# Decayed block attention ahead of two gated feed-forward stages: products of 64x64x64 in the four quarters of TensorE's array

## The chip, the cores and the metric

The kernel runs on one core of a Trainium2 chip. The metric is the time of one execution on the device, in microseconds (us). TensorE (PE) multiplies, VectorE (DVE) and ScalarE (ACT) move results out of its accumulators (PSUM), GpSimd (POOL) does element-wise work between buffers, SyncE (SP) issues the large loads, and 16 DMA engines carry them. "PEld" in a row is PE's load of the stationary operand.

## What is computed

The first part is a decayed attention over blocks of 64 tokens, with a running state per head; its output is the input of a gated feed-forward stage and of a stage of eight experts. Only the first part is touched. Cut to that part, the reference is:

```
B, H, S, D = 2, 8, 768, 64            # block = 64
Dmask = where(rel >= 0, lam ** rel, 0)            # rel = i - j inside a block
for b in range(S // 64):
    intra = (q_b @ k_b.T * Dmask) @ v_b
    inter = (q_b * lam ** (i + 1)) @ kv_state
    out_b = intra + inter
    kv_state = lam ** 64 * kv_state + (k_b * lam ** (63 - i)).T @ v_b
x = out in rows of H * D = 512                    # 1536 tokens
x = (silu(x @ w_gate) * (x @ w_val)) @ w_out
out = experts(x)
```

## The kernel before

The kernel is one program without a loop; the order of the code is the order of each engine's queue (`tc.manual_schedule()`). The attention walks over 12 **units**. A unit is a chunk of 128 tokens of one of the two batches, all 8 heads; units of the two batches alternate. Since a decayed recurrence may be cut at any block length, the kernel uses blocks of 128 tokens. Heads are handled in four pairs; a pair fills 128 rows (2 heads x 64).

For a unit:

- `load` (L227) fetches q, k and v, each 128 tokens x 8 heads x 64 values, 256 KB, by one DMA from SP's queue (L233; k of unit 0 in two halves). Each of the three has 5 buffers. The load of unit u+5 stands at the end of iteration u.
- `em_T` (L285) transposes q and k pair by pair on PE (L295), ACT copies the result out (L297, tile `tT`), DVE scales q by the powers of lam (L301, `qd`), and POOL scales k (L304, `kd`).
- `em_S` (L307) forms the scores of each head (L315: 64 rows of the array, 128 columns), and DVE multiplies them by the decay mask (L318, tiles `at0`, `at1`), two times 512 wide.
- `em_O` (L325) forms the update of the state (L332, `pu`), the state's part of the output (L343) and the scores' part (L347: 128 rows, 64 columns of the array) in one bank `po`. ACT writes the high part of the output `x1[0]` (L353), DVE the rest `x1[1]` (L356) and the new state (L361, L363), of which only the two diagonal 64x64 blocks of each pair are kept; POOL prepares `tmp`, the old state times lam (L335).

All these operands are f32, and a product of f32 shows as two MATMULs and two LDWEIGHTS in the trace. The main loop runs T(u+1), O(u), S(u+1) for the first five units, then T(u+2), S(u+1), O(u). In units 5, 7, 9, 11 the calls `bg_begin()` and `bg(n)` interleave the preparation of the first weights of the feed-forward stage: steps L166, L153, L159, L160, L173 rebuild f32 from the words of a wider type, L141 and L149 split them in a high and a low part. `pump_dma` (L102) fetches one further piece of weights (512 KB). The decay mask `dec` and the powers `lrep` come from two scans on DVE (L260, L269), whose inputs are `lam_b` (lam on all partitions) and `lam_s` (lam of the pair's head on each half of the partitions); three DMAs from ACT's queue bring these (L238, L240), a fourth `wr`, the router's weights.

After the last unit `em_GV` begins: 24 MATMULs of 128x512 per block (L204), 12 for the gate, 12 for the value, first over the 512 first tokens of batch 0. It needs the prepared pieces of weights, and from then on PE works without a gap.

Of the kernel before, what the change touches and what calls it, by code (L numbers as in the profile page):

```python
# [20 lines left out]
def decayed_attention_two_moes(  # L21
# [14 lines left out]
    nc = tc.nc  # L36
# [176 lines left out]
    lam_s = const.tile([P, NP], F32, name="lam_s")  # L213
# [7 lines left out]

    att = ExitStack()
    ap = att.enter_context(tc.tile_pool(name="ap", bufs=1, side="right", reuse_waits="tile"))
    units = [(c, b) for c in range(NCH) for b in range(B)]
    qkv = {}

    def load(u):  # L227
        c, b = units[u]
        for n, src in enumerate((q, k, v)):
            t = ap.tile([P, H, D], F32, tag=f"in{n}", name=f"in{n}", bufs=5)  # L230
            w = H // 2 if u == 0 and n == 1 else H
            for h in range(0, H, w):
                nc.sync.dma_start(out=t[:, h:h + w, :],  # L233
                                  in_=src[b, h:h + w, c * P:(c + 1) * P, :].rearrange("h s d -> s h d"))
            qkv[u, n] = t

    load(0)
# [6 lines left out]
    load(1)  # L244
    load(2)
    load(3)
    load(4)
    nc.scalar.dma_start(out=wr, in_=w_router.rearrange("(k p) e -> p k e", p=P))


    dec = ap.tile([P, 2, NP, P], F32, name="dec")
    lrep = ap.tile([P, NP, P], F32, name="lrep")
    d0 = rawp.tile([P, 2, NP, P], F32, tag="raw", name="raw")
    d1 = rawp.tile([P, 2, NP, P], F32, tag="raw", name="raw")
    nc.vector.tensor_copy(out=d0, in_=lam_b.rearrange("j (p x) -> j x p", x=2).unsqueeze(3).to_broadcast([P, 2, NP, P]))
    nc.vector.memset(d0[:, :, :, 0:1], 0.0)
    for x in range(2):
        nc.gpsimd.tensor_copy(out=d1[:, x], in_=ident.unsqueeze(1).to_broadcast([P, NP, P]))
    flat = "j x p i -> j (x p i)"
# [4 lines left out]
    d2 = rawp.tile([P, 2, NP, P], F32, tag="raw", name="raw")  # L264
    nc.vector.memset(d2[:, 1], 0.0)
    nc.vector.tensor_copy(out=d2[:, 1, :, 0:1], in_=lam_s.unsqueeze(2))
    nc.vector.tensor_copy(out=d2[:, 0], in_=lam_s.unsqueeze(2).to_broadcast([P, NP, P]))
    nc.vector.memset(d2[:, 0, :, 0:1], 0.0)
    nc.vector.tensor_tensor_scan(  # L269
        out=lrep.rearrange("j p i -> j (p i)"),  # L270
        data0=d2[:, 0].rearrange("j p i -> j (p i)"), data1=d2[:, 1].rearrange("j p i -> j (p i)"),
        initial=0.0, op0=ALU.mult, op1=ALU.add,
    )
    St = [ap.tile([P, NP, P], F32, name=f"st{b}") for b in range(B)]
    for b in range(B):
        nc.gpsimd.memset(St[b], 0.0)

    qT, kT, qd, kd, att_w = {}, {}, {}, {}, {}
    cnt = {"t": 0, "s": 0, "o": 0}
    rev = dec[:, :, :, P - 1].rearrange("j x p -> j p x").unsqueeze(3).to_broadcast([P, NP, 2, D])  # L280

    def pair(t, p):
        return t[:, 2 * p:2 * p + 2, :].rearrange("s h d -> s (h d)")

    def em_T(u):  # L285
        c, b = units[u]
        for n in range(2):
            pt = bank(cnt["t"] % 2).rearrange("p (a b) -> p a b", a=NP)
            cnt["t"] += 1
            t = ap.tile([P, NP, P], F32, tag=f"tT{n}", name=f"tT{n}", bufs=2)  # L290
            w = NP // 2 if u == 0 and n == 1 else NP
            for p in range(NP):
                if p == w:
                    pt = bank(7).rearrange("p (a b) -> p a b", a=NP)
                nc.tensor.transpose(pt[:, p, :], pair(qkv[u, n], p), ident)  # L295
                if p % w == w - 1:
                    nc.scalar.copy(out=t[:, p + 1 - w:p + 1, :], in_=pt[:, p + 1 - w:p + 1, :])  # L297
            (qT, kT)[n][u] = t
            if n == 0 and c > 0:
                qd[u] = ap.tile([P, NP, P], F32, tag="qd", name="qd", bufs=3)  # L300
                nc.vector.tensor_tensor(out=qd[u], in0=t, in1=lrep, op=ALU.mult)  # L301
        if c < NCH - 1:
            kd[u] = ap.tile([P, H, D], F32, tag="kd", name="kd", bufs=2)
            nc.gpsimd.tensor_tensor(out=kd[u].rearrange("s (p x) d -> s p x d", x=2),  # L304
                                    in0=qkv[u, 1].rearrange("s (p x) d -> s p x d", x=2), in1=rev, op=ALU.mult)

    def em_S(u, conv):  # L307
        pss = []
        for x in range(2):
            pss.append(bank(2 + cnt["s"] % 3).rearrange("p (a b) -> p a b", a=NP))  # L310
            cnt["s"] += 1
        for p in range(NP):
            for x in range(2):
                r = slice(x * D, (x + 1) * D)
                nc.tensor.matmul(pss[x][:, p, :], lhsT=kT[u][r, p, :], rhs=qT[u][r, p, :], start=True, stop=True)  # L315
        for x in range(2):
            t = ap.tile([P, NP, P], F32, tag=f"at{x}", name=f"at{x}", bufs=2)
            nc.vector.tensor_tensor(out=t, in0=pss[x], in1=dec[:, x], op=ALU.mult)  # L318
            att_w[u, x] = t
# [675 lines left out]
```

## Time and profile before

| what | value |
|---|---|
| median of 3 runs | 591.12 us (590.98 to 591.58) |
| the profiled execution | 590.82 us, of it the traced span 589.0 us |
| PE busy, share of the span | 561.8 us, 95% |
| DVE | 392.5 us, 67% |
| ACT | 241.6 us, 41% |
| POOL | 102.9 us, 17% |
| MATMULs | 3202 |

The profiled execution is 1.8 us longer than its span, and 0.3 us shorter than the median. The span has three stages: the attention up to the first L204 at 73.7 us, the feed-forward and expert stages up to about 577 us, and the last stores. A share of busy time over the whole span says little of the first stage, which is read by itself.

### The profile page before, as it was taken

Reading aid. Unit: us, or ns where it says so; the run is one execution under the profiler, and the core shown is the slowest. Engines: PE = TensorE matmul, PEld = TensorE weight load, DVE = VectorE, ACT = ScalarE, POOL = GpSimd, SP = SyncE. Lnnn points to the kernel's source line nnn. Section 1 sums busy time; section 2 is a strip of 40 time slices with the busy share of each in tenths; the row PEclk is TensorE's granted clock in tenths of the full one; section 3 lists DMA queues with packets and bytes.
Section 4 is the critical chain, followed back from the end, with each engine's and each line's share of the span. In section 5 each row is a group of like instructions: output and inputs, shape, how many; then the busy total and the mean of one; then the engine's idle time right before and its main releaser. Section 6 shows DMA issues by size and latency. Waiting matters only on the chain.

```text
span 589.0 us, 8506 instructions
## 1 busy us (share of the span) xinstructions
PE 561.8 (95%) x3202; PEld 465.6 (79%) x3202; DVE 392.5 (67%) x778; ACT 241.6 (41%) x434; POOL 102.9 (17%) x102
## 2 busy tenths in 40 slices
PE   4999999999999999999999999989999999999991
PEld 3888888888888888888888888678888888888881
DVE  4577799888414888562586467886868887777530
ACT  2343244443332444300343333234767666666420
POOL 3325200000000000000000013313265245142001
PEclk9999999999999999999999999999999999999996
DMA  7999132322220322220122176327697677660000
GB/s 130 203 242 215 38 108 107 108 92 88 74 69 0 108 85 95 71 72 0 35 75 101 41 251 195 112 106 232 156 303 247 207 264 238 198 204 28 0 25 31
DMA packets 84011, 72.97 MB, mean 124 GB/s; under 512 B 43228, under 2 KB 69852, under 8 KB 83968
## 3 DMA queue, kind: packets, MB, share of 16 engines
q1 hardware_dynamic: 78128, 65.02, 37.1%
q0 software_dynamic: 3072, 7.35, 3.7%
q8 instruction: 26, 0.43, 0.3%
q10 hardware_dynamic: 2768, 0.03, 0.3%
q14 instruction: 17, 0.14, 0.1%
HBM read 66.09 MB, written 7.08 MB: 124 GB/s over the span
## 4 chain that ended last, share of the span: by engine, by line
PE 77%; issue 10%; DMA 5%; DVE 4%; POOL 2%; ACT 1%; SPq 0%; POOLq 0%; ACTq 0%; DVEq 0%
PE b L204 58%; PE b L629 6%; PE b L630 3%; DMA in<-in_q_dram 2%; PE b L347 2%; PE b L332 2%; PE b L315 1%; PE b L295 1%; PE b L343 1%; DMA gg<-gd,g_idx 1%; POOL out_dram L674 1%; POOL xg L594 1%; PE b L512 1%; DMA xg<-x2d,g_first 1%; DMA in<-in_k_dram 1%
## 5 line engine op out<-in xcount | busy, mean ns | idle before, releaser
L204 PE MATMUL b<-x,w 128*128 128x512 f32 x864 | 199.6, 394 | 0.0
L204 PEld LDWEIGHTS b<-x,w 128*128 128x128 f32 x864 | 162.7, 188 | 36.3 <-issue 0.2
L204 PE MATMUL b<-w,hT 128*128 128x512 f32 x432 | 105.0, 398 | 0.0
L204 PE MATMUL b<-w,h 128*128 128x512 f32 (+1 forms) x384 | 101.0, 398 | 0.0
L204 PEld LDWEIGHTS b<-w,hT 128*128 128x128 f32 x432 | 79.9, 188 | 18.2
L629 PE MATMUL b<-xT,w 128*128 128x480 f32 x224 | 77.0, 383 | 0.1
L204 PEld LDWEIGHTS b<-w,h 128*128 128x128 f32 (+1 forms) x384 | 65.1, 183 | 14.7 <-ACT h L636 0.4
L630 PE MATMUL b<-xT,w 128*128 128x240 f32 x224 | 61.3, 274 | 0.0
L464 ACT CAST hT<-th 128x512 fp32r<-128x512 f32 x36 | 22.4, 622 | 87.3 <-DVE th L462 87.3
L629 PEld LDWEIGHTS b<-xT,w 128*128 128x128 f32 x224 | 42.1, 188 | 9.0 <-DVE hs L634 1.1
L460 DVE SCALAR_TENSOR_TENSOR th<-th,b 128x512 f32<-128x512 f32 x36 | 24.8, 688 | 33.8 <-ACT th L459 33.8
L630 PEld LDWEIGHTS b<-xT,w 128*128 128x128 f32 x224 | 42.5, 190 | 2.3
L504 POOL TENSOR_TENSOR xt<-xr,xt 128x512 bf16<-128x512 f32 x12 | 14.0, 1163 | 173.5 <-ACT xt L503 173.5
L459 ACT ACTIVATE th<-b 128x512 f32<-128x512 f32 x36 | 21.5, 598 | 55.3 <-PE b L204 55.3
L674 POOL DMA_INDIRECT out_dram<-y,s_idx x16 | 27.1, 1696 | 92.8 <-ACT y L673 74.0
L637 DVE SCALAR_TENSOR_TENSOR h<-hs,h 128x240 fp32r<-128x240 f32 x56 | 22.9, 409 | 26.4 <-ACT h L636 26.4
L149 DVE TENSOR_TENSOR w<-acc,w 128x1024 fp32r<-128x1024 f32 x32 | 38.9, 1221 | 1.5 <-ACT w L141 1.5
L462 DVE SCALAR_TENSOR_TENSOR th<-th,b 128x512 f32<-128x512 f32 x36 | 24.7, 687 | 19.1 <-PE b L204 19.1
L636 ACT ACTIVATE h<-hs 128x240 fp32r<-128x240 f32 x56 | 22.7, 405 | 34.6 <-DVE hs L634 34.6
L149 DVE TENSOR_TENSOR w<-raw,w 128x1024 fp32r<-128x1024 f32 x28 | 34.3, 1228 | 3.7 <-ACT w L141 3.4
L141 ACT CAST w<-acc 128x1024 fp32r<-128x1024 f32 x32 | 33.1, 1045 | 2.8 <-DMA raw<-in_moe_w_dram 2.7
L634 DVE TENSOR_TENSOR hs<-b,hs 128x240 f32<-128x240 f32 x56 | 22.6, 404 | 17.1 <-ACT hs L633 16.9
(133 smaller groups left out, 676.4 us busy)
## 6 DMA issues: line engine op xcount, KB each, us to landing
acc<-in_moe_w_dram SPq DMA_DIRECT2D x32, 512.0 KB, 4.4
raw<-in_moe_w_dram SPq DMA_DIRECT2D x28, 512.0 KB, 4.5
raw<-in_moe_w_gate_dram SPq DMA_DIRECT2D x12, 512.0 KB, 3.5
raw<-in_moe_w_val_dram SPq DMA_DIRECT2D x12, 512.0 KB, 3.5
raw<-in_moe_w_out_dram SPq DMA_DIRECT2D x12, 512.0 KB, 3.2
in<-in_q_dram SPq DMA_DIRECT2D x12, 256.0 KB, 5.0
in<-in_v_dram SPq DMA_DIRECT2D x12, 256.0 KB, 5.2
x2d<-acc SPq DMA_DIRECT2D x12, 256.0 KB, 3.3
```

Source lines behind the costliest of these rows:

```text
L141: nc.scalar.copy(out=w[:, 0:n], in_=x)
L149: nc.vector.tensor_tensor(out=lo, in0=x, in1=hi, op=ALU.subtract)
L204: nc.tensor.matmul(acc, lhsT=a[x], rhs=b[y], start=first and n == 0, stop=last and n == 2)
L460: nc.vector.scalar_tensor_tensor(out=th, in0=th, scalar=1.0, in1=pg, op0=ALU.add, op1=ALU.mult)
L462: nc.vector.scalar_tensor_tensor(out=th, in0=th, scalar=0.5, in1=pv, op0=ALU.mult, op1=ALU.mult)
L464: nc.scalar.copy(out=hh[:, 0], in_=th)
L629: nc.tensor.matmul(ph, lhsT=hi, rhs=xt[:, kk], start=kk == 0, stop=kk == KD - 1, skip_group_check=True)
L630: nc.tensor.matmul(ph[:, 0], lhsT=lo, rhs=xt[:, kk, 0], start=False, stop=kk == KD - 1, skip_group_check=True)
L634: nc.vector.tensor_tensor(out=hs, in0=ph[:, 0], in1=hs, op=ALU.add)
L636: nc.scalar.activation(out=hh[:, 0], in_=hs, func=ACTF.Relu)
L637: nc.vector.scalar_tensor_tensor(out=hh[:, 1], in0=hs, scalar=0.0, in1=hh[:, 0].bitcast(F32), op0=ALU.max, op1=ALU.subtract)
L674: put = nc.gpsimd.indirect_dma_start(out=out, out_offset=bass.IndirectOffsetOnAxis(ap=si[0:m], axis=0), in_=y[0:m], in_offset=None, bounds ...
```

## The change

The chunk inside a unit becomes 64 tokens, so a unit holds two blocks, h = 0 and 1, with a state update between them. Head H is addressed as (r, j) with r = H // 4: head j of group r; a transposed pair is (0, j) over (1, j), so that the group r is also the half of the partitions. Every product but the transposes is 64x64x64 and names a quarter of the array: its rows by the half of the partitions that the operands lie on, its columns by the half that the result lies on; products of different row halves go to different banks. The state is 64 wide instead of 128 (`St`, `sth`, `tmp`: 128 x 256 values). Six buffers for q, k, v instead of five; q and k are loaded in halves of four heads each. `lam_s` and its two DMAs are gone, `wr` is fetched after the loop. Weights are prepared by a whole `tick()` at the end of units 6, 8 and 10, and two pieces each are fetched after units 0 and 3. The output banks 6 and 7 are the same for every unit.

```diff
-    lam_s = const.tile([P, NP], F32, name="lam_s")
...
+    L = P // 2
+    NJ = H // 2
...
+    DEEP = 6
     def load(u):
...
+            if n < 2:
+                t = t.rearrange("s (j r) d -> s r j d", r=2)
+                for r in range(2):
+                    nc.sync.dma_start(out=t[:, r], in_=src[:, r * NJ:(r + 1) * NJ, :])
+            else:
+                nc.sync.dma_start(out=t, in_=src)
...
     nc.scalar.dma_start(out=lam_b, in_=lam.unsqueeze(0).to_broadcast([P, H]))
-    for x in range(2):
-        nc.scalar.dma_start(
-            out=lam_s[x * D:(x + 1) * D, :],
-            in_=lam.rearrange("(p x) -> x p", x=2)[x:x + 1, :].to_broadcast([D, NP]),
-        )
...
-    nc.scalar.dma_start(out=wr, in_=w_router.rearrange("(k p) e -> p k e", p=P))
+    for u in range(DEEP):
+        load(u)
...
+    def em_pu(u):
+        c, b = units[u]
+        xb[u] = [bank(2 + 2 * (u % 2) + r).rearrange("p (n j i) -> p n j i", n=2, j=NJ) for r in range(2)]
+        for j in range(NJ):
+            for h, r in quarters():
+                if h == 0 or c < NCH - 1:
+                    nc.tensor.matmul(xb[u][h][half[r], 1, j, :], lhsT=kd[u][half[h], r, j, :],
+                                     rhs=qkv[u, 2][half[h], r, j, :], start=True, stop=True)
+
+    def em_S(u):
+        for j in range(NJ):
+            for r, h in quarters():
+                nc.tensor.matmul(xb[u][r][half[h], 0, j, :], lhsT=kT[u][half[r], j, h, :], rhs=qT[u][half[r], j, h, :],
+                                 start=True, stop=True)
+
+    def em_mask(u):
+        for r in range(2):
+            t = ap.tile([P, NJ, L], F32, tag=f"at{r}", name=f"at{r}", bufs=2)
+            nc.vector.tensor_tensor(out=t, in0=xb[u][r][:, 0], in1=dec[:, r], op=ALU.mult)
...
+    def em_state(u, h):
...
+            nc.gpsimd.tensor_tensor(out=tmp, in0=old, in1=lam_L, op=ALU.mult)
+            nc.vector.tensor_tensor(out=new, in0=tmp, in1=xb[u][h][:, 1], op=ALU.add)
...
+    def em_inter(u, h, old, first):
+        for jj in range(2):
+            for r, x in quarters():
+                j = 2 * jj + x
+                nc.tensor.matmul(ob[u][r][half[x], jj, half[h]], lhsT=old[half[r], j, :], rhs=qd[u][half[r], j, h, :],
...
+    def em_intra(u, swap, first):
+        for jj in range(2):
+            for h, x in quarters():
+                j, r = 2 * jj + x, h ^ swap
+                nc.tensor.matmul(ob[u][r][half[x], jj, half[h]], lhsT=qkv[u, 2][half[h], r, j, :],
+                                 rhs=at_w[u, r][half[h], j, :], start=first and jj == 0, stop=bool(swap),
...
+    def em_O(u):
+        ob[u] = [bank(6 + r)[:, 0:2 * P].rearrange("p (j s) -> p j s", j=2) for r in range(2)]
+        old = before.pop(u)
+        if old is not None:
+            em_inter(u, 0, old, True)
+        em_intra(u, 0, old is None)
+        em_inter(u, 1, sth[u], False)
...
+    def em_products(u):
+        before[u] = St.get(units[u][1])
+        em_pu(u)
+        em_S(u)
+        em_mask(u)
+        em_state(u, 0)
...
     for u in range(NU):
+        nxt = u + 1 < NU
+        em_O(u)
+        em_hi(u, 0)
+        if nxt:
+            em_products(u + 1)
+        em_intra(u, 1, False)
+        em_hi(u, 1)
+        em_lo(u)
+        if nxt:
+            em_state(u + 1, 1)
+        if u + 2 < NU:
+            em_kd(u + 2)
+            em_T(u + 2)
+            em_qd(u + 2)
+        if u in (6, 8, 10):
+            tick()
+        if u + DEEP < NU:
+            load(u + DEEP)
+        if u in (0, 3):
             pump_dma()
             pump_dma()
+    nc.scalar.dma_start(out=wr, in_=w_router.rearrange("(k p) e -> p k e", p=P))
```

`em_hi(u, swap)` copies a half of each output bank on ACT (two copies of 128 x 2 x 64), `em_lo(u)` writes the low parts on DVE (two, 128 x 2 x 128), `em_T` transposes on PE and copies on ACT as before, `em_qd` and `em_kd` scale q and k as before.

How the queues change, first PE. Before, from the transposes of unit 3 into the products of unit 2 (a row is a product, "x4" four in a row):

```order
L295 MATMUL b_294<-ident,in_120 128x128 x4
L295 MATMUL b_303<-ident,in_122 128x128 x4
L332 MATMUL b_312<-in_118,kd 128x128 x4
L343 MATMUL b_319<-qd,st_148 128x128 x4
L347 MATMUL b_319<-at_284,in_118 64x128
L347 MATMUL b_319<-at_286,in_118 64x128
```

Now, from the last scores of unit 4 (L318) over the last products of unit 3 and the transposes of unit 5 into the first products of unit 4:

```order
L318 MATMUL b_481<-tT_434,tT_441 64x64 x2
L318 MATMUL b_482<-tT_434,tT_441 64x64 x2
L357 MATMUL b_454<-at_405,in_120 64x64 x2
L357 MATMUL b_453<-at_403,in_120 64x64 x2
L357 MATMUL b_454<-at_405,in_120 64x64 x2
L357 MATMUL b_453<-at_403,in_120 64x64 x2
L293 MATMUL b_541<-ident,in_130 128x128 x4
L293 MATMUL b_548<-ident,in_133 128x128 x4
L350 MATMUL b_565<-qd,st 64x64 x2
L350 MATMUL b_566<-qd,st 64x64 x2
```

The products are a quarter of the size and four times as many; between the scores of a unit and the first use of its output banks stand eight products and the transposes.

DVE's queue over one unit, before (`at` is the masked score, `x_1` the low part of the output, `st` the state):

```order
L318 TENSOR_TENSOR at_346<-b_336,dec 128x512
L318 TENSOR_TENSOR at_348<-b_337,dec 128x512
L301 TENSOR_TENSOR qd<-tT_361,lrep 128x512
L356 TENSOR_TENSOR x_1_94<-b_385,x_0_93 128x4x128
L363 TENSOR_TENSOR st_149<-tmp,b_378 64x4x64 x2
```

and now:

```order
L324 TENSOR_TENSOR at_515<-b_481,dec 128x256
L324 TENSOR_TENSOR at_517<-b_482,dec 128x256
L339 TENSOR_TENSOR st<-tmp,b_481 128x256
L385 TENSOR_TENSOR x_1_93<-b_453,x_0_92 128x2x128
L385 TENSOR_TENSOR x_1_93<-b_454,x_0_92 128x2x128
L339 TENSOR_TENSOR st<-tmp,b_482 128x256
L299 TENSOR_TENSOR qd<-tT_546,lrep 128x512
```

The low parts of the output of unit 3 (banks 453, 454) now stand behind the two masks and the first state of unit 4, and the product of unit 4 that writes these banks anew (565 and 566 are the same two banks) waits for them.

## Rows read from the trace of the kernel before

**Rows 1.** Stretches: busy us of PE, PEld, DVE, ACT, POOL; granted clock, DMA share, GB/s.
```profile
16.30:73.70 57.40, 54.44 (x601) 47.60 (x600) 39.98 (x71) 19.37 (x35) 21.32 (x29) 1.00 0.79 173
73.70:575.00 501.30, 497.23 (x2556) 410.29 (x2555) 345.16 (x696) 217.67 (x391) 74.72 (x59) 1.00 0.37 120
```

**Rows 2.** Timeline of the first weight blocks and the end of the attention.
```profile
72.97 0.42 DVE L159 TENSOR_SCALAR cv<-cv 128x512 uint32<-128x512 uint32 x1
73.42 0.69 DVE L160 SCALAR_TENSOR_TENSOR cv<-raw,cv 128x512 uint32<-128x512 uint32 x1
73.73 6.47 PE L204 MATMUL b<-x,w 128*128 128x512 f32 x27
75.35 0.28 DVE L425 TENSOR_SCALAR tri<-iota_c,part 128x128 f16<-128x128 f32 x1
```

**Rows 3.** Timeline of one unit: start, us, engine, line, count, idle before.
```profile
24.66 1.13 PE L332 MATMUL b<-in,kd 128*128 128x128 f32 x8 [0.25 <-PE b L295]
25.63 1.06 PE L343 MATMUL b<-qd,st 128*128 128x128 f32 x8
26.61 1.09 PE L347 MATMUL b<-at,in 128*64 128x128 f32 x16
27.64 1.16 PE L315 MATMUL b<-tT,tT 64*128 64x128 f32 x16
27.75 0.58 ACT L353 CAST x<-b 128x512 fp32r<-128x512 f32 x1 [2.61 <-PE b L347]
28.37 0.69 DVE L356 TENSOR_TENSOR x<-b,x 128x512 fp32r<-128x512 f32 x1 [2.05 <-ACT x L353]
28.73 1.09 PE L295 MATMUL b<-ident,in 128*128 128x128 f32 x8
28.98 0.86 DVE L363 TENSOR_TENSOR st<-tmp,b 64x256 f32<-64x256 f32 x2
30.09 1.13 PE L332 MATMUL b<-in,kd 128*128 128x128 f32 x8 [0.27 <-DVE st L363]
```

**Rows 4.** Timeline of PE cut to narrow windows, two places of the trace.
```profile
26.61 0.33 PE L347 MATMUL b<-at,in 128*64 128x128 f32 x2
...
347.89 0.48 PE L522 MATMUL b<-wr,xt 128*128 128x24 bf16 x12
```

**Rows 5.** Group by line and shape, whole span: count, busy us, mean ns.
```profile
L522 PE MATMUL b<-wr,xt 128*128 128x24 bf16 x144 | 5.5, 173 | 0.0
```

**Rows 6.** Groups by line and shape, 0 to 74.5 us: count, busy, mean ns.
```profile
L318 DVE TENSOR_TENSOR at<-b,dec 128x512 f32<-128x512 f32 x24 | 15.5, 685 | 0.3
L297 ACT COPY tT<-b 128x512 f32<-128x512 f32 x23 | 12.6, 587 | 13.6 <-PE b L295 13.6
L304 POOL TENSOR_TENSOR kd<-in,dec 128x512 f32<-128x512 f32 x10 | 12.0, 1200 | 35.9 <-DMA in<-in_k_dram 11.6 <-PE b L332 11.6 <-issue 9.4
L363 DVE TENSOR_TENSOR st<-tmp,b 64x256 f32<-64x256 f32 x16 | 6.6, 413 | 0.2
L297 ACT COPY tT<-b 128x256 f32<-128x256 f32 x2 | 0.8, 375 | 2.8 <-PE b L295 2.8
```

**Rows 7.** Timeline of the first microseconds.
```profile
4.10 0.69 DVE L255 COPY raw<-lam_b 128x1024 f32<-128x1024 f32 x1 [3.24 <-DMA lam_b<-in_lam_dram]
4.66 1.51 PE L295 MATMUL b<-ident,in 128*128 128x128 f32 x6 [4.66 <-DMA in<-in_q_dram]
5.05 2.29 DVE L260 TENSOR_TENSOR_SCAN dec<-raw 128x1024 f32<-128x1024 f32 x1
9.37 2.08 PE L315 MATMUL b<-tT,tT 64*128 64x128 f32 x16
```

**Rows 8.** Stretches again, two early ones; GB/s of the loads stand last.
```profile
4.00:9.00 5.00, 1.76 (x7) 1.39 (x8) 3.54 (x4) 0.86 (x2) 0.12 (x1) 1.00 0.31 58
9.00:20.00 11.00, 9.77 (x74) 8.04 (x73) 4.62 (x10) 2.64 (x6) 3.05 (x3) 1.00 1.25 220
```

**Rows 9.** ACT's DMA queue from 4 to 9 us: packets, MB, share of 16 engines.
```profile
q10 hardware_dynamic: 607, 0.01, 5.8%
```

More of the change, by code (lines that the diff above doesn't have):

```diff
@@ L224, in decayed_attention_two_moes @@
     units = [(c, b) for c in range(NCH) for b in range(B)]
+    NU = len(units)
+    DEEP = 6
     qkv = {}
+    half = [slice(x * L, (x + 1) * L) for x in range(2)]
     def load(u):
@@ L229, in load @@
         for n, src in enumerate((q, k, v)):
[L230 to L234, printed above, removed]
+            t = ap.tile([P, H, D], F32, tag=f"in{n}", name=f"in{n}", bufs=DEEP)
+            src = src[b, :, c * P:(c + 1) * P, :].rearrange("h s d -> s h d")
@@ new lines, in decayed_attention_two_moes @@
+    dec = ap.tile([P, 2, NJ, L], F32, name="dec")
+    lrep = ap.tile([P, NJ, L], F32, name="lrep")
+    d0 = rawp.tile([P, 2, NJ, L], F32, tag="raw", name="raw")
+    d1 = rawp.tile([P, 2, NJ, L], F32, tag="raw", name="raw")
+    d2 = rawp.tile([P, 2, NJ, L], F32, tag="raw", name="raw")
+    lam_rj = lam_b.rearrange("p (r j) -> p r j", r=2)
+    for h in half:
+        nc.gpsimd.tensor_copy(out=d1[h].rearrange("p r j i -> p (r j) i"),
+                              in_=ident[h, h].unsqueeze(1).to_broadcast([L, H, L]))
@@ L263, in decayed_attention_two_moes @@
     )
[L264 to L267, printed above, removed]
+    for r in range(2):
+        lam_r = lam_rj[half[r], r].unsqueeze(2)
+        nc.vector.tensor_copy(out=d2[half[r], 0], in_=lam_r.to_broadcast([L, NJ, L]))
+        nc.vector.tensor_copy(out=d2[half[r], 1, :, 0:1], in_=lam_r)
@@ L275, in decayed_attention_two_moes @@
[L275 to L283, printed above, removed]
-    def em_T(u):
-        c, b = units[u]
[L287 to L319, printed above, removed]
-            if conv:
-                bg(1 + x)
-        qT.pop(u)
-        kT.pop(u)
@@ new lines, in decayed_attention_two_moes, with quarters @@
+    lam_L = lrep[:, :, L - 1:L].to_broadcast([P, NJ, D])
+    St, sth, qT, kT, qd, kd, xb, at_w, ob = {}, {}, {}, {}, {}, {}, {}, {}, {}
+    def quarters():
+        return [(a, b) for a in range(2) for b in range(2)]
+    def em_T(u):
+        for n, got in enumerate((qT, kT)):
+            pt = bank(n).rearrange("p (j s) -> p j s", j=NJ)
+            for j in range(NJ):
+                nc.tensor.transpose(pt[:, j, :], qkv[u, n][:, :, j, :].rearrange("s r d -> s (r d)"), ident)
+            got[u] = ap.tile([P, NJ, 2, L], F32, tag=f"tT{n}", name=f"tT{n}", bufs=2)
+            nc.scalar.copy(out=got[u].rearrange("p j h i -> p j (h i)"), in_=pt)
+        qd[u] = ap.tile([P, NJ, 2, L], F32, tag="qd", name="qd", bufs=3)
@@ new lines, in decayed_attention_two_moes, with em_hi @@
+    before = {}
+    def em_O(u):
[6 more added lines that the diff above has]
+        em_inter(u, 1, sth[u], False)
+    def em_hi(u, swap):
+        c, b = units[u]
+        for r in range(2):
+            s0 = b * S + c * P + (r ^ swap) * L
+            nc.scalar.copy(out=x1[0][:, 2 * r:2 * r + 2, s0:s0 + L], in_=ob[u][r][:, :, half[r ^ swap]])
@@ new lines, in em_lo @@
+    def em_lo(u):
+        c, b = units[u]
+        s0 = b * S + c * P
+        for r in range(2):
+            hi = x1[0][:, 2 * r:2 * r + 2, s0:s0 + P]
+            nc.vector.tensor_tensor(out=x1[1][:, 2 * r:2 * r + 2, s0:s0 + P], in0=ob[u][r], in1=hi.bitcast(F32),
+                                    op=ALU.subtract)
+    def em_products(u):
[4 more added lines that the diff above has]
+        em_state(u, 0)
+    em_kd(0)
+    em_T(0)
+    em_qd(0)
```

112 lines of the change are left out of this document (33 added, 79 removed).

## The prediction

> **What bounds the kernel now.** I first split the span by stage [rows 1]. From 73.7 us on, PE is busy 497.2 of 501.3 us; nothing of the change reaches in there, so that stage stays as long as it is, and the change is worth what the first L204 moves away from 73.73 us [rows 2]. In the attention proper PE is busy 54.4 of 57.4 us at the full granted clock, DVE 40, POOL 21, ACT 19 [rows 1]: PE is the bound. The timeline of a unit shows how [rows 3]: L332, L343, L347, L315 and L295 follow each other, the next L332 begins 5.43 us after the last (24.66 to 30.09). A MATMUL of 128 columns that holds the whole array takes 0.11 us (the eight of L343, 0.98 us from their start to the next group's); those that hold half of it come in pairs: 16 of L347 or L315 take as long as 8 of L343. So the halves of the array work side by side already, and 8 whole plus 16 half MATMULs are equal work.
>
> **The size of a quarter product.** A row for it doesn't exist; it is bounded. The window of 0.03 us on L347 holds two MATMULs that end 0.33 us after the first began [rows 4], so two on different parts of the array start almost together. If four quarters do that too, each needs half of the 0.11 us, since it streams 64 columns instead of 128: four MATMULs in 55 ns, 14 ns each. If only two overlap: 28 ns. If none: 55 ns. Below 14 ns nothing can go, the columns must pass. I take 14, since row halves (L315) and column halves (L347) each overlap fully and a quarter is one of each, and the code gives the two row halves different banks. On issue: twelve MATMULs of 24 columns, each on the whole array, take 0.48 us to the end of the last [rows 4]; one lasts 0.173 [rows 5], so they start 28 ns apart. The Trainium skill ("TensorE: Matmul & The Clock Gate", section "Wait — 56ns, not 53.3ns?") states that the start-to-start time never falls below about 25 ns, however few the columns; by that the sum would be some 12 us worse (rival 1). The pair of L347 speaks against it for different parts of the array.
>
> **PE per unit, after.** 16 products each for state update and scores, 8 each for two inter and two intra groups: 64 products, 128 MATMULs; before there were 48, and 8 transposes in both. At 14 ns, 16 MATMULs take 0.22 us: 8 x 0.22 = 1.8 us, with transposes (1.09, [rows 3]) 2.9 instead of 5.4 us. PE stops being the bound.
>
> **What is late next: a loop through DVE.** The output banks 6 and 7 exist once, so the first product of unit u+1 on them waits for both low parts (L385) of unit u, and these stand on DVE behind the masks and the first state of u+1. From the end of the scores: 0.05 us to DVE (PE to ACT, L347 to L353, [rows 3]); five steps 256 wide at 0.43 (0.413 by L363, 256 wide too, plus a gap; [rows 6]) = 2.15; 0.25 back to PE (L363 ends at 29.84, L332 begins at 30.09, [rows 3]): 2.45 us. Inside it lie, free of charge: intra (0.22) and transposes (1.09), and ACT's two late high copies. These are 128 wide, a little under the 0.375 of 256 [rows 6], at the slope of 0.375 to 0.587 some 0.27 each; they end 0.8 us after the scores, before the low parts' turn at 1.35. Then inter, intra, inter, update and scores, 7 x 0.22 = 1.55, plus 0.15 for the start: **4.15 us per unit** against 5.43. DVE's own work is six steps of 0.43 and `qd` at 0.69 [rows 6], 3.3 us. POOL has 1.2 for `kd` and two halves of that for `tmp`, 2.4; ACT 2 x 0.59 + 4 x 0.27 = 2.3. All fit. The 80 extra MATMULs' loads of weights run beside them, as L347's do.
>
> **Start.** lam_b lands at 4.1; a 512-wide copy and scan, half of 0.69 and 2.29 [rows 7], give `dec` at 5.8, then `kd` 7.0. PE is at half pace that early: 16 of L315 take 2.08 at 9.4 us against 1.16 later [rows 3, 7]. That is the pace of the lower of its two clock levels, 1.2 instead of 2.4 GHz, though the rows' granted clock reads 1.00 [rows 8]. Update and scores of unit 0, 0.9 each, end at 8.8, transposes of unit 1 (2.0: six take 1.51 at that pace, [rows 7]) at 10.8, its first outputs at 11.7, unit 1's scores at 13.5; unit 1's first product on the banks after 2.45 more: 16. Ten periods later, 57.5, unit 11 begins. The tick after unit 8 puts four conversion steps (two of 0.42, two of 0.69 by [rows 2]) in DVE's queue, 2.2 us, of which 0.85 fit in its gap: 58.9. Unit 11's 64 MATMULs 0.9 + 0.15: the first L204 at **59.9**.
>
> **The loads.** A second line with nearly the same end. Twelve units of three times 262 KB and four pieces of 524 KB are 11.5 MB; the stream runs at 220 GB/s when it is full [rows 8]: 52.4 us, from about 2 us on: last v at 54.4, last k 1.2 earlier, 53.2. Then transposes 1.1 at most, 0.6 ACT, scores 0.45, the DVE loop 2.45, unit 11: 1.05: 58.9. SP's halves move the same bytes and packets in five issues instead of three. This holds only if the hole from 4 to 9 us goes, where the loads moved 58 GB/s while 607 tiny packets of ACT's queue (q10) trickled [rows 8, 9]. I take these to be mostly `lam_s`, which goes, and `wr`, which comes later. If the hole stays, it costs 5 x (220 - 58) / 220 = 3.7 us on this line.
>
> **Behind the attention.** The tick after unit 10 (2.9 us of DVE with L149) delays the low part of the second weight piece: low outputs at 58.7, tick 61.7, unit 11's low parts 62.6, L425 0.28, L149 as long as L160, 0.69 [rows 2]: 63.6. PE's gate needs 12 x 0.24 (6.47 / 27, [rows 2]) = 2.9, so its third value MATMUL would come at 63.3: 0.3 us lost.
>
> **Sum.** 73.7 - 59.9 = 13.8 less 0.3: 13.5 us off the profiled 590.8 (its span 589.0 and 1.8 around it) = 577.3. The median is 0.3 above that execution; I say 577.6.
>
> **Rivals.**
> 1. *Every MATMUL keeps a start-to-start time of its own, whatever its quarter*: 28 ns by L522 [rows 4, 5]. The 112 in the loop take 3.1 instead of 1.55 us, period 5.7: unit 11 at 16 + 57 = 73, then 64 x 28 = 1.8 and 0.15, the tick hidden in DVE's longer gap: 75.2, so 592. By the skill's 25 ns it would be 589. The pair of L347, at most 10 ns apart, speaks against it. Chance 0.10.
> 2. *Only two quarters side by side, or PE, now idle 1.1 us in each period, falls to its lower clock level.* Both double the products to 28 ns (at the lower clock the transposes take 2.2 and just fill the 2.45): 592 again. For it: the halved pace of the first 16 us [rows 7]; against it nothing direct for the clock, since PE never idled so regularly before. Chance 0.11.
> 3. *Quarters one at a time* (place: the array; price: 55 ns per MATMUL). Period 2.45 + 6.2 + 0.15 = 8.8, last unit 3.5: 17.5 + 88 + 3.5 = 109, so 626. It decides from 26 ns per MATMUL, where 16 + 10 x (2.6 + 112 t) + 64 t + 0.15 reaches 73.7: above that the kernel is slower than before. Against it: halves overlap. Chance 0.06.
> 4. *The lam loads weren't the cause of the hole*: loads end 3.7 later, first L204 at 62.6, 580. Part of the first case. *Faster than forecast* (loads above 220 GB/s and no loss behind the attention): 571, chance 0.04 below 571.
>
> **Numbers.** Forecast with its neighbours, 571 to 585: 0.68; below: 0.04; 585 to 589.9 (cases 1 and 2 in part): 0.07; within 0.2% (1.2 us, about what a measurement here can tell): 0.08; slower by more: 0.13 (the rest of cases 1 and 2, and 3). So faster 0.79, same 0.08, slower 0.13. The range 571 to 591 leaves out 0.04 below and some 0.15 above.
>
> **What would show it.** Right: the 16 MATMULs of a group of 64x64 products in about 0.25 us plus their length, units 4 to 4.3 us apart, PE waiting for L385 before L350, no hole in the loads at 4 to 9 us, L204 from about 60 us, and the stages behind unchanged. Wrong: groups of 64x64 at 25 ns or more per MATMUL; a granted clock or pace at half; PE waiting for `in` loads in most units; a first L204 later than 70 us; gaps among the L204.

## The result and the profile after

| | before | after |
|---|---|---|
| median of 4 runs each, same chip | 591.35 us (590.98 to 592.37) | 584.21 us (581.13 to 584.74) |
| ratio | | 0.9866, 95% interval 0.9829 to 0.9903 |
| profiled execution | 590.82 us, span 589.0 | 584.74 us, span 582.9 |
| first L204 (the stage behind the attention begins) | 73.73 us [rows 2] | 68.75 us |

The kernel is faster by 7.1 us, where 13.5 were forecast; the time lies in the forecast range. Span against span it is 6.1 us, and these come from three places: the first L204 stands 5.0 us earlier, the twelve MATMULs from there lose 2.2 us, and what follows, from the twelfth L204 to the end of the span, is 3.4 us shorter (509.30 against 512.66).

**What came as forecast.** The hole in the loads is gone. A stretch of the changed kernel (busy us and count of PE, PEld, DVE, ACT, POOL; then granted clock, DMA share, GB/s), to be read against [rows 8]:

```profile
4.00:9.00 5.00, 4.18 (x73) 3.35 (x74) 4.38 (x10) 1.17 (x2) 1.07 (x1) 1.00 1.30 227
```

227 GB/s instead of 58 from 4 to 9 us. One unit in the timeline of the changed kernel (start, duration, engine, line, count, idle before):

```profile
15.92 0.69 PE L312 MATMUL b<-in,kd 64*64 64x64 f32 x32 [0.37 <-POOL kd L303]
...
18.59 0.72 PE L350 MATMUL b<-qd,st 64*64 64x64 f32 x14 [0.25 <-DVE x L385]
...
19.80 0.28 PE L357 MATMUL b<-at,in 64*64 64x64 f32 x3 [0.31 <-issue]
...
20.63 0.62 PE L318 MATMUL b<-tT,tT 64*64 64x64 f32 x28
...
21.33 0.76 DVE L324 TENSOR_TENSOR at<-b,dec 128x256 f32<-128x256 f32 x2 [0.86 <-PE b L318]
...
22.00 0.41 DVE L339 TENSOR_TENSOR st<-tmp,b 128x256 f32<-128x256 f32 x1
22.33 0.75 DVE L385 TENSOR_TENSOR x<-b,x 128x256 fp32r<-128x256 f32 x2
22.80 0.71 PE L350 MATMUL b<-qd,st 64*64 64x64 f32 x13
```

The 32 MATMULs of L312 end 0.69 us after the first began; one lasts about 0.23, which leaves 0.46 / 31 = 15 ns from start to start on average: four quarters do work side by side. The steps of the forecast loop are there: scores, two masks (L324), state (L339), two low parts (L385), the next L350, 4.21 us after the last, and 4.05 in the unit before. But L350 starts at 22.80, before the pair of L385 ends (22.33 + 0.75 = 23.08): it waits for the first low part only. And the first row shows PE waiting for POOL's `kd`. Experiment 4 comes back to both.

**What did not.** In the middle of a group of equal products PE stops, and nothing in the profile is what it waits for. Timeline of PE in the changed kernel:

```profile
40.69 0.28 PE L357 MATMUL b<-at,in 64*64 64x64 f32 x3
42.83 0.45 PE L357 MATMUL b<-at,in 64*64 64x64 f32 x13 [1.87 <-issue]
```

Three of the 16 intra products ran, and 13 stood for 1.87 us although their operands were the same. There are seven such stops, from the 0.31 us at 19.80 above to 1.59 at 53.07 us. PE's waits by cause from 4 to 70 us (line, cause: us in total, times, longest):

```profile
PE b L293 <- DMA in<-in_q_dram: 4.6, 1, 4.6
PE b L350 <- DVE x L385: 4.5, 5, 2.7
PE b L357 <- issue: 4.0, 4, 1.9
PE b L293 <- issue: 2.2, 1, 2.2
PE b L318 <- issue: 1.6, 1, 1.6
...
PE b L350 <- issue: 1.0, 1, 1.0
```

8.8 us of "issue", none of it in the kernel before. The instruction queue has grown with the products; DMA traffic by queue from 4 to 58 us (packets, MB, share), before:

```profile
q8 instruction: 4, 0.07, 0.6%
```

and after:

```profile
q8 instruction: 10, 0.16, 1.5%
```

The clock fell too. Stretches of the changed kernel, columns as above:

```profile
40.00:45.00 5.00, 3.13 (x90) 2.60 (x81) 2.42 (x8) 1.42 (x5) 2.78 (x4) 0.84 0.91 193
...
50.00:55.00 5.00, 3.27 (x113) 2.96 (x103) 2.49 (x6) 1.02 (x5) 1.80 (x3) 0.87 0.97 198
...
60.00:65.00 5.00, 2.65 (x112) 2.33 (x112) 3.61 (x9) 0.72 (x4) 2.25 (x14) 0.89 0.33 108
65.00:70.00 5.00, 3.76 (x67) 3.23 (x68) 4.71 (x12) 2.87 (x10) 0.00 (x0) 0.50 0.00 0
```

And the tick after unit 8 costs more than its steps. PE's wait for L385 there, the next one, and the stage's first products, PE in the timeline:

```profile
62.13 0.72 PE L350 MATMUL b<-qd,st 64*64 64x64 f32 x14 [2.66 <-DVE x L385]
65.87 0.91 PE L350 MATMUL b<-qd,st 64*64 64x64 f32 x14 [1.09 <-DVE x L385]
...
68.75 5.49 PE L204 MATMUL b<-x,w 128*128 128x512 f32 x12
```

and DVE just before:

```profile
58.16 1.56 DVE L160 SCALAR_TENSOR_TENSOR cv<-raw,cv 128x512 uint32<-128x512 uint32 x1
...
60.67 0.74 DVE L324 TENSOR_TENSOR at<-b,dec 128x256 f32<-128x256 f32 x2
```

L160 takes 1.56 us beside POOL's `kd` and `tmp`, where it took 0.69 [rows 2]. Twelve of L204 take 5.49 us at the lower clock level (granted 0.50, which is 1.2 GHz); from the first one's start to the twelfth's that is 4.86 us, and 2.65 before.

**Behind the attention** the same MATMULs became cheaper. The 48th to the 1101st L204, busy us, in the kernel before:

```profile
84.62:327.88 243.26, 243.26 (x1055) 198.12 (x1053) 1.00 0.23 74
```

and in the changed one:

```profile
82.12:322.63 240.51, 240.51 (x1054) 197.73 (x1053) 1.00 0.22 73
```

2.75 us less with PE busy all of the time and the clock at 1.00 in both. The change touches no instruction there; it moves addresses. `lam_s` lay in the constants' pool, and without it every tile on the left side (weights, `x1`, `raw`) lies 32 bytes lower, while `hT`, on the right, stays: in the built programs the first weight tile begins at byte 21760 before and 21728 after, `hT` at 151520 in both.

### The profile page after: what moved, and what is told of

It is laid out like the page before. It is cut to its first block, busy times and chain, and to the rows that moved or that the text cites. A ratio compares the mean times of both kernels' runs of the same rounds, so it can differ in the third digit from the quotient of the medians.

```text
span 582.9 us, 10450 instructions
## 1 busy us (share of the span) xinstructions
PE 546.9 (94%) x4130; PEld 454.1 (78%) x4130; DVE 392.3 (67%) x796; ACT 245.9 (42%) x469; POOL 110.8 (19%) x114
## 4 chain that ended last, share of the span: by engine, by line
PE 76%; issue 10%; POOL 5%; DVE 4%; DMA 2%; ACT 1%; POOLq 0%; SPq 0%; DVEq 0%; ACTq 0%
PE b L204 61%; PE b L658 6%; PE b L659 3%; PE b L684 2%; POOL tmp L338 2%; POOL kd L303 2%; DMA in<-in_k_dram 1%; POOL out_dram L703 1%; PE b L642 1%; PE b L541 1%; DMA xg<-x2d,g_first 1%; DVE oi L567 1%; DMA lam_b<-in_lam_dram 0%; DVE xr L531 0%; ACT xt L530 0%
## 5 line engine op out<-in xcount | busy, mean ns | idle before, releaser
L204 PE MATMUL b<-x,w 128*128 128x512 f32 x864 | 200.9, 395 | 0.0
L204 PEld LDWEIGHTS b<-x,w 128*128 128x128 f32 x864 | 164.0, 190 | 36.2
L204 PE MATMUL b<-w,hT 128*128 128x512 f32 x432 | 102.8, 393 | 0.0
L204 PE MATMUL b<-w,h 128*128 128x512 f32 (+1 forms) x384 | 101.1, 399 | 0.0
L204 PEld LDWEIGHTS b<-w,hT 128*128 128x128 f32 x432 | 79.9, 188 | 16.1
L204 PEld LDWEIGHTS b<-w,h 128*128 128x128 f32 (+1 forms) x384 | 65.1, 182 | 15.0 <-ACT h L665 0.4
L141 ACT CAST w<-acc 128x1024 fp32r<-128x1024 f32 x32 | 33.2, 1045 | 2.8 <-DMA raw<-in_moe_w_dram 2.7
```

What stands on the lines that cost most here:

```text
L141: nc.scalar.copy(out=w[:, 0:n], in_=x)
L204: nc.tensor.matmul(acc, lhsT=a[x], rhs=b[y], start=first and n == 0, stop=last and n == 2)
```

## The experiments

Two theories stood at the start. **A**: the gain comes from what goes with `lam_s` (the small loads, and the addresses), and the quarter products earn nothing on balance, because their instructions are fetched too slowly. **B**: the quarters earn it, and the pauses are a small loss on a large gain. Each chip has its own runs of the kernel before beside it, so ratios are compared.

### 1. The kernel before without the small loads

```diff
-    for x in range(2):
-        nc.scalar.dma_start(out=lam_s[...], in_=lam...)
+    for x in range(2):
+        nc.vector.tensor_copy(out=lam_s[x * D:(x + 1) * D, :], in_=lam_b[...][:, x, :])
...
-    nc.scalar.dma_start(out=wr, ...)      # before the loop
+    nc.scalar.dma_start(out=wr, ...)      # after it
```

> The kernel before with one part of the change alone: lam_s is copied from lam_b by two small copies on DVE instead of two DMAs, and wr is fetched after the attention loop. All addresses stay. Theory 1 (the tiny loads make the hole of 4 to 9 us): the stretch 4 to 9 us carries about 200 GB/s instead of 58, unit 0 and 1 begin some 3 us earlier, PE-bound from there, so the first L204 comes at 70 to 71 us and the time is 588 (3 us less). Rival (the hole has another cause, or the first units wait for something else): still under 100 GB/s there, time within 1 us of before.

Measured: 587.18 us against 592.35, ratio 0.9919 (0.9901 to 0.9937). The stretch of the loads, and the stage's first products:

```profile
4.00:9.00 5.00, 4.13 (x25) 3.54 (x26) 4.58 (x8) 1.23 (x3) 1.06 (x1) 1.00 1.31 229
```

```profile
68.98 3.25 PE L204 MATMUL b<-x,w 128*128 128x512 f32 x13
```

The hole was these DMAs, and without one quarter product the stage begins at 68.98 us, within 0.3 us of the changed kernel's 68.75. That is more than theory 1 expected, 4.75 us earlier than before and 5.2 us of time instead of 3. Of the 607 packets of [rows 9] 508 carry 4 bytes (`lam_s`) and 99 carry 32 (`wr`); no run takes the two apart.

### 2. The kernel before, `lam_s` in another pool

```diff
-    lam_s = const.tile([P, NP], F32, name="lam_s")
...
+    lam_s = ap.tile([P, NP], F32, name="lam_s")
```

> The kernel before with lam_s moved out of the pool of constants into the attention's pool, nothing else: every weight tile, x1 and raw lies 32 bytes lower, as they do after the change. Theory 2 (the 3.8 us that the changed kernel gained behind the attention come from these addresses): MATMULs of the group w,hT follow each other after 227 ns instead of 233, the first L204 stays at 73.7 us, and the time is 587.3, 3.5 to 4 us less. Rival (they come from the order of transfers or from the clock): within 1 us of before.

Measured: 588.88 us, ratio 0.9939 (0.9922 to 0.9955). The same 1054 products of L204:

```profile
84.32:324.79 240.47, 240.47 (x1054) 197.73 (x1053) 1.00 0.23 75
```

Nothing but addresses moved, and the stretch takes 240.47 us as in the changed kernel. Most of it lies in the products of weights with `hT`: from start to start they take 226.9 ns (227.0 in the changed kernel) instead of 233.3.

### 3. The changed kernel with a pad in `lam_s`' place

```diff
+    pad = const.tile([P, NP], F32, name="pad")
+    nc.vector.memset(pad, 0.0)
```

> The changed kernel with a tile of 16 bytes in the place of lam_s, so that all addresses left of the attention are those of the kernel before. Theory 2: 588, 3.5 to 4 us more than the changed kernel, with 233 ns in the group w,hT; so only 2 to 4 us of the change's gain come from the attention itself. Rival: the same time as the changed kernel, 584.

Measured: 587.58 us (583.86 to 591.12), ratio 0.9904 (0.9871 to 0.9937). The stretch is back at the price of before:

```profile
79.51:322.75 243.24, 243.24 (x1054) 197.90 (x1053) 1.00 0.22 72
```

So the two experiments agree from both sides: 32 bytes are worth 2.8 us in this stretch. In the time of the whole kernel the pad does not show clearly, since this interval overlaps the changed kernel's. Why the bytes matter is not shown; no run looked at another shift.

### 4. The changed kernel without the loads of units 6 to 11

```diff
-            load(u + DEEP)
+            for n in range(3):
+                qkv[u + DEEP, n] = qkv[u, n]
```

> The changed kernel without the loads of units 6 to 11; these units compute with the q, k and v of units 0 to 5. Theory 3 (PE's pauses inside a group of equal products, 8.8 us in sum, are waits for its own instructions, which come in packets of 16 KB about 4.4 us apart, and the full DMA queues make that slow): with the queues empty from about 25 us on the packets come sooner, most pauses behind 27 us are gone, units 4.2 us apart up to unit 8, and the first L204 at 60 to 62 us. If the packets are slow by themselves, the pauses stay at 1 to 2 us each. Rival (the pauses are waits for q and k): they are gone too, but the packets' times are unchanged. Where PE pauses no longer, the granted clock should stay at 1.00 up to unit 9.

Measured: 580.3 us in one run, first L204 at 65.39. PE's timeline:

```profile
29.74 0.38 PE L350 MATMUL b<-qd,st 64*64 64x64 f32 x9 [1.77 <-issue]
34.40 0.38 PE L293 MATMUL b<-ident,in 128*128 128x128 f32 x2 [1.83 <-issue]
43.31 0.72 PE L350 MATMUL b<-qd,st 64*64 64x64 f32 x14 [0.25 <-DVE x L385]
47.35 0.72 PE L350 MATMUL b<-qd,st 64*64 64x64 f32 x14 [0.25 <-DVE x L385]
51.41 0.72 PE L350 MATMUL b<-qd,st 64*64 64x64 f32 x14 [0.25 <-DVE x L385]
58.45 0.86 PE L350 MATMUL b<-qd,st 64*64 64x64 f32 x14 [3.26 <-DVE x L385]
```

While loads run, the pauses are there as before; the last packet of the loads ends at 33.2 us, the last pause at 34.40, and from there on there is none. Instruction packets still come, about every 3.7 us. So the pauses need the loads. How the loads hold up the fetch is not shown: a packet takes 0.94 to 1.18 us without them and 1.01 to 1.99 beside them in the changed kernel, and the trace has no time at which it was asked for.

Units now follow each other every 4.04 and 4.06 us, near the forecast 4.15, but not by the forecast loop. The chain of work that ended last, in the window from 36 to 66 us (start, us, what), comes round like this:

```profile
44.69 0.69 PE b L312 x32
45.38 0.48 PE b L318 x32
...
46.23 0.41 DVE at L324
46.64 0.34 DVE st L339
...
47.05 0.62 POOL tmp L338
47.67 1.03 POOL kd L303
...
48.74 0.69 PE b L312 x32
```

From the state it runs over two steps of POOL, `tmp` and `kd`, into the next update, 4.05 us later; L312 waits 0.14 us for `kd`. The low parts and the banks are not on it.

The unit with the tick then takes 7.04 us (51.41 to 58.45), and the clock falls behind it. PE waits there for L385, so this part has nothing to do with fetching. The first L204 missed the 60 to 62 us that were expected: without a pause after 34.40 it still comes 5.5 us later than the 59.9 forecast.

### 5. The kernel before with both by-products

Experiments 1 and 2 together.

> The kernel before with both by-products of the change and no quarter products: the small loads of lam_s and of the router's weights gone (lam_s copied out of lam_b), and the lam_s tile out of the constants' pool, so that the tiles on the left side lie 32 bytes lower. Theory A (the quarter products earn nothing on balance): the two gains add, ratio to before 0.984 to 0.988, the same as the changed kernel in this call; first L204 (of the stage GV) near 69 us, its products 227 ns apart. Rival (the quarters earn the larger part, and the two single runs overstated what their edits are worth): ratio 0.990 or more, over 2 us behind the changed kernel.

### 6. The changed kernel once more

> The changed kernel once more, unaltered, as the measure for the others on the same chip: ratio 0.983 to 0.990, first L204 near 68.7 us, pauses of PE inside groups of equal products of 8 to 9 us in the loop. If the pauses or the falls of the clock lie elsewhere in this execution by more than 2 us, their places are chance, and only their sum can be compared.

Measured on one chip: number 5 took 583.34 us, ratio 0.9856 (0.9834 to 0.9877); number 6 585.06 us, ratio 0.9878 (0.985 to 0.9905), both against 591.96. The kernel before with its attention untouched, but for a pool and a few small loads, is as fast as the changed one. Number 5 has its first L204 at 69.02 us, and its stretch of 1054 products takes 240.5 us. Theory A holds in its result, B falls: the quarters, the compact state and the new loop are worth nothing that these runs can tell from zero. One part of the expectation of number 6 missed: its pauses came to 5.7 us in the waits, not 8 to 9, so their sum changes from one execution to the next; the changed kernel's times spread over 4.8 us here, while those of number 5 stay within 1.4. The reason that A gave, the fetch, is only one part of the loss, as number 4 shows.

### 7. The changed kernel without the inter products

```diff
-        if old is not None:
-            em_inter(u, 0, old, True)
-        em_intra(u, 0, old is None)
-        em_inter(u, 1, sth[u], False)
+        em_intra(u, 0, True)
```

> The changed kernel without em_inter: the products of the old states with the decayed queries are left out of the output, some 64 of PE's 272 records per unit; loads, DVE, ACT and POOL do the same work as before. Theory A (PE's pauses inside groups of equal products come from the number of its instructions, which are fetched 256 at a time past full load queues): fewer packets of the instruction queue until 58 us (7 instead of 9) and pauses of under 4 us in place of 8.8 us; first L204 at 62 to 66 us. Rival 1 (the pauses come with the loads whatever PE issues): 7 to 9 us of pauses remain. Rival 2 (with less work PE's granted clock falls sooner): under 0.8 of the clock in 40 to 65 us, first L204 at 68 us or later.

Measured: 581.26 us in one run, first L204 at 64.95. PE's waits from 4 to 70 us:

```profile
PE b L293 <- DMA in<-in_q_dram: 9.6, 3, 4.7
PE b L312 <- POOL kd L303: 4.3, 8, 0.6
...
PE b L293 <- DMA in<-in_k_dram: 1.9, 2, 1.4
PE b L318 <- issue: 1.1, 1, 1.1
```

and one of the waits for `kd` in its timeline:

```profile
20.01 0.69 PE L312 MATMUL b<-in,kd 64*64 64x64 f32 x32 [0.60 <-POOL kd L303]
```

With 208 records per unit instead of 272 the pauses shrink from 8.8 (5.7 in number 6) to 1.1 us under the same loads: they hang on the number of PE's instructions as well. The first units show it best: up to 27 us the loads run as fast as in the changed kernel (193 against 185 GB/s from 16 to 27 us) and the units follow every 4.05 us, and there is no pause where the changed kernel has two. Later PE also stands in other waits, in which a fetch could catch up. The period of 4.05 us is the same with fewer products because POOL's `kd` sets it: L312 now waits 0.60 us for it in these units. Only part of the time comes back, 3.8 us at the first L204. The first 4.7 us of waiting for q is the start; the other 6.8 us of waiting for q and k (9.6 + 1.9 - 4.7) are new: the loop now runs into the line of the loads. The pauses had been covering it. And the clock falls here too (granted 0.60 from 55 to 60 us).

### 8. The ticks spread

```diff
-        if u in (6, 8, 10):
-            tick()
+        if u == 9:
+            bg_begin()
+        for n in {5: (1,), 6: (0,), 7: (1,), 8: (2,), 9: (0,), 10: (1, 2)}.get(u, ()):
+            bg(n)
```

> The changed kernel with the three whole ticks after units 6, 8 and 10 taken apart: the same steps in the same order, but one or two after each of the units 5 to 10. Theory A (in the loop through DVE a whole tick between two units stands on the path, and the long wait that it makes lets the clock fall): the stretch from unit 9's to unit 10's first product on the banks falls from 6.54 to about 4.8 us, the wait of 2.66 us there to under 1 us, first L204 at 64 to 67 instead of 68.75 us, and 2 to 5 us less than the changed kernel in this call. Rival (GpSimd's and ACT's steps are the cost wherever the pieces stand, or the fetch of instructions fills the gap): the first L204 within 1 us of 68.75 and no measurable gain.

> The changed kernel with the ticks spread once more, unaltered, as the measure for the two on the same chip: ratio to before 0.983 to 0.987, first L204 at 66 to 67.5 us.

Measured: 583.4 us, ratio 0.9851 (0.9827 to 0.9874), on the chip of numbers 5 and 6; the repetition on another chip 579.87 us, ratio 0.9816 (0.9786 to 0.9845). PE in the first of them:

```profile
59.91 0.72 PE L350 MATMUL b<-qd,st 64*64 64x64 f32 x14 [0.21 <-DVE x L385]
...
66.80 3.52 PE L204 MATMUL b<-x,w 128*128 128x512 f32 x9
```

The wait of 2.66 us before unit 10 is 0.21, and its period 4.8 us; the first L204 comes at 66.80 and 67.54 us against 68.11 in number 6. In the repetition PE works through the last unit at a granted clock of 1.00:

```profile
65.45 0.72 PE L350 MATMUL b<-qd,st 64*64 64x64 f32 x14 [1.29 <-DVE x L385]
...
67.54 2.80 PE L204 MATMUL b<-x,w 128*128 128x512 f32 x11
```

In time the step from 0.9878 to 0.9851 lies within the intervals: theory A is right on the place, and the gain is not shown.

### 9. The raw loads later

Number 8 with its pieces one unit later, and:

```diff
-        if u in (0, 3):
+        if u in (3, 5):
             pump_dma()
             pump_dma()
```

> The changed kernel with the ticks spread, and the four loads of raw expert weights (1 MB before unit 7's loads, 1 MB before unit 10's) issued later, behind the loads of units 9 and 11; the pieces of the ticks stand one unit later. Theory A (where the fetch pauses leave room, the loads of q, k, v are what the loop waits for next): units 7 to 9 get their tiles some 5 us earlier, unit 11's some 2.5 us; first L204 at 63 to 66 us instead of 66.8 and 1 to 3 us less than the version with the ticks spread alone. Rival 1 (with the load queues as full as before, the pauses at the packets of PE's instructions set the pace whatever the order of the loads): first L204 at 66 to 68 us, no gain. Rival 2 (the raw pieces come too late for the ticks, whose first step on ACT then holds the copies behind it): a wait of 2 us or more on ACT for the raw tile, first L204 at 69 us or later, slower than the spread alone.

Measured: 579.65 us, ratio 0.98 (0.9773 to 0.9826); number 8 on the same chip 579.87. The first L204 moved as far as theory A said:

```profile
64.13 6.08 PE L204 MATMUL b<-x,w 128*128 128x512 f32 x19
```

That is 3.4 us earlier than number 8's 67.54 on this chip. Part of it can be chance: PE's pauses came to 7.9 us here and to 10.6 there, and no run takes the two apart. The whole kernel gained 0.2 us, which is nothing. Part was given back at once: the twelfth L204 stands at 68.21 against 70.17 (the granted clock is 0.77 from 65 to 70 us against 1.00). These 2.0 us are still there at the 1101st (316.94 against 318.93), and 0.4 us at the last (565.51 against 565.92). What took them in the stages between, where L204 has gaps, stays open. It is the fastest version of this study; its interval lies below the changed kernel's two, on another chip.

### 10. Filler products against the clock

Number 9 and:

```diff
+    def em_fill(n):
+        for _ in range(n):
+            nc.tensor.matmul(bank(0), lhsT=x1[0][:, 0, 0:P], rhs=x1[0][:, 0, 0:4 * P], start=True, stop=True)
...
+        if not nxt:
+            em_fill(2)
         em_intra(u, 1, False)
...
+        if u == NU - 2:
+            em_fill(4)
```

> The version with later raw loads, and six products of 512 columns whose result nobody reads, four of them in PE's wait before unit 11's first product on the banks and two before the last unit's last group. Theory A (PE's idle stretches at the end of the loop lower the clock that GV starts with): granted clock of 0.9 or more in 66 to 70 us (0.66 with the ticks spread), first twelve L204 in 2.7 to 3.0 us instead of 3.8 us, 1 us less in time. Rival (the products come late for the wait that they fill and push unit 11 back): first L204 0.5 us or more later than without them, no gain.

Measured: 580.55 us, ratio 0.9811 (0.9783 to 0.9839). PE's timeline:

```profile
64.93 2.17 PE L363 MATMUL b<-x 128*128 128x512 f32 x4
...
69.27 6.00 PE L204 MATMUL b<-x,w 128*128 128x512 f32 x25
```

The granted clock from 65 to 70 us is 1.00 and the stage starts at full pace (25 MATMULs in 6.00 us). That the fillers did it is not shown: the repetition of number 8, without them, also had 1.00 there, and its first twelve L204 took 2.63 us from start to start against 2.64 here. The rival's part did happen: a filler takes 0.55 us and not the 0.23 of an L204, the four stand 2.17 us in a wait that was 1.3 in number 9, and the first L204 comes 5.1 us later than there, in an execution with 3.3 us more of pauses (11.2 in all). No gain.

## Why the prediction was right in sign and too large

Right, by its steps: **the size of a quarter product** (14 ns forecast, 15 measured, so neither 25 to 28 ns, rival 1, nor one quarter at a time, rival 3). It was worked out from 0.11 us for a whole product; the 0.98 us for eight in [rows 3] make 0.12, and by the same steps 15 ns. The Trainium skill's floor ("TensorE: Matmul & The Clock Gate", section "Wait — 56ns, not 53.3ns?") doesn't bind across quarters: the trace disagrees, with those 15 ns. **The hole in the loads**: it was `lam_s` and `wr`, as taken; rival 4 is out by experiment 1. **The loads' line** is there, as experiment 7 shows, and 4 us later than worked out: SP issued the last v at 54.27 us, and the last packet of the stream ended at 58.4, not 54.4; the stream from 4 to 58 us averaged 210 GB/s, not 220.

Right in its number, by luck: **the loop through DVE**, 4.15 us forecast, 4.04 to 4.06 in experiment 4, and 4.05 to 4.33 in the first units. The 2.45 us from the end of the scores to the next product on the banks were 1.5 (45.86 to 47.35 in experiment 4), because that product waits for the first low part and not for both, and because DVE's steps follow each other after 0.33 us and not 0.43. From that product to the end of the next scores it took 2.55 us (43.31 to 45.86) and not 1.70. In that part PE waits for `kd`, which comes round by the chain over POOL of experiment 4. The step "POOL has 1.2 for `kd` ... All fit" looked at POOL as a sum of work (2.4 us forecast, 0.62 + 1.06 + 1.07 = 2.75 in the undisturbed units) that fits into the period, not as a link of the loop. The loop through the banks alone would be at about 3.9 us, an estimate: 4.05 less the 0.14 that L312 waits for `kd`.

Wrong, and by how much. The first L204 was to stand at 59.9 us and stood at 68.75, 8.85 later: 1.5 gained at the start, 8.5 lost in the units, 1.8 in the last of them. In the order of the sum:

- **The start** was 1.5 us better than its step: unit 1's first product on the banks came at 14.5 us, not 16. The scores of unit 1 ended at 13.03 us instead of 13.5, and the 2.45 behind them were 1.5 here too. PE was at half pace less long than taken: 32 products of L312 take 1.13 us at 7.00 and 0.69 at 11.87. The trace's record of the granted clock begins at 9.29 us (16.96 in the kernel before), so a 1.00 ahead of that is no measurement.
- **"PE stops being the bound ... All fit"** failed. The step costed PE's products by their columns (a record below is a MATMUL or the load of its weights) and the loading of their weights at nothing, and left out that each is an instruction that has to be fetched: some 272 records per unit instead of 112. From unit 1 to unit 11 the units took 51.3 us, where ten periods and the tick's term make 42.9: 8.5 us too many. The four periods with the pauses of 1 us and more are 7.65 us over 4.15 in sum, unit 10's with the tick is 2.4 over, and the other five are 0.2 under; two of the four also hold a fall of the clock. Experiments 4 and 7 show that the pauses need both, many instructions and running loads. Where they stand shows what they are: in the changed kernel PE pauses after its 706th, 961st, 1218th, 1473rd, 1730th, 1985th and 2497th record, always 255 to 257 or twice that apart, and in the eight other traces of it and of its versions every pause stands on the same row of numbers, which goes on over 2242, 2754 and 3009. In time, the pause that ends at 42.83 us ends 1.4 us after the end of a 16 KB packet of the instruction queue (begun at 40.09, 1.3 us long), and the other six end 1.3 to 1.7 us after such a packet. The Trainium skill ("Runtime: NRT & Kernel Launch", section "Instruction fetch mechanics") says that instructions come in 16 KiB blocks of 256 and that crossing into the next is mostly hidden: the block agrees with the 33 packets and 0.54 MB of the profile's page and with the 256 records from pause to pause, and that it is hidden held for the kernel before, with no pause at 4 packets, but not here with 10.
- **The tick's term** was 1.35 us and too small: unit 10's period was 6.54 us, 2.4 above 4.15. The step took each conversion at its duration in [rows 2], with POOL idle; beside `kd` and `tmp` L160 took 1.56 us instead of 0.69. The row to read was in the trace of before: its L160 at 55.52 us, with POOL busy on `kd`, takes 1.43 us.
- **The clock**, a part of rival 2, did not come from PE's regular idling of 1.1 us per period: in the undisturbed units of experiment 4 the granted clock stays 1.00 from 38.4 to 58.9 us, though PE idles in each; in the changed kernel it falls behind the stops that end at 42.83, 53.07 (pauses) and 62.13 us (the tick). No run changes the stops alone, so that they are the cause is argued from this order. The fall cost the first twelve L204 2.2 us (4.86 instead of 2.65), and the last unit some 0.8.
- **The last unit** was 2.88 us long (65.87 to 68.75) instead of 1.05. At a clock of 1.00 it takes 2.09 us (65.45 to 67.54 in the repetition of experiment 8), so 1.04 were missing in the step itself: it counted 64 products back to back, and left out among others that the last group waits for ACT's high copies of the group before (L378, 0.45 us).
- **"That stage stays as long as it is"** failed in the other direction: from the twelfth L204 on it is 3.4 us shorter, of which 2.75 lie in the stretch measured above and are a matter of addresses; the rest was not traced to a cause. The 0.3 us forecast as lost behind the attention can't be made out beside that.

So the 13.5 us shrank by 8.85 and 2.2 and gained 3.4 and the 0.3 back: 6.1, the 6.1 us between the spans. The division of the credit failed too: the hole was taken for 3.7 us on the loads' line and the quarters for the rest. By experiment 1 the hole alone moves the first L204 from 73.73 to 68.98 us, with the old products at their old pace; the quarters' faster loop then met the fetch, `kd`, the tick, the clock and, behind these, the loads, and brought it to 68.75.

## What to carry to other kernels

Cutting products into smaller ones multiplies instructions, so count instructions per microsecond beside columns, and look for waits named "issue" in the middle of a group of equal products while loads run. An engine whose work fits into the period can still be a link of the loop that sets it, so follow every chain round before adding up. When a change earns what was forecast, undo its by-products one at a time: here a few hundred tiny packets and 32 bytes of pool gave as much as the whole change. A line that is taken away uncovers the next, so before paying for a faster loop ask when its last load lands.

## What the runs showed of the hardware that was not expected

- Products on four quarters of the array start 15 ns apart on average, 32 in 0.69 us.
- PE's pauses for its instructions stand 255 to 257 records apart (or a multiple of it), at the same counts from the start in all nine traces of the changed kernel and its versions.
- The same MATMULs of L204 took 243.3 or 240.5 us for 1054 of them, by whether the tiles on the left lay 32 bytes higher or lower, in six traces: 243.26, 243.24 and 243.26 (before, experiments 3 and 1) against 240.51, 240.47 and 240.51 (after, experiments 2 and 5). Experiments 4, 6, 8, 9 and 10, at the lower addresses too, took 240.47 to 240.51; experiment 7, which leaves the inter products out, took 241.68, since its products of `x` were slower, and why is open.
- DVE's L160 on 128x512 words took 1.56 us (before: 1.43) where POOL ran elementwise steps beside it and 0.69 where POOL was idle, 73.42 us in the kernel before.
- Fillers (experiment 10): each took 0.55 us, L204 0.23 to 0.24, both at a granted clock of 1.00. A filler lasts 0.50 us and the next begins 0.06 us after its end, where each L204 begins before the one before has ended. The fillers all write the same bank anew, so that each may wait for the last; that was not tried.
